# Other step numbers for weight sums, operand rows and output-weight conversions in the feed-forward part of a bucketed attention kernel

## The chip, the cores and the metric

The kernel runs on one core of one Trainium2 chip. The metric is the device time of one execution in microseconds; of the kernel before there are three timed runs and one profiled execution.

## What is computed

Four batches, eight heads, 768 positions of 64 dimensions go through an attention in which a query sees only the keys of its own hash bucket, and the 3072 resulting rows of 512 numbers go through two matrix products with a piecewise activation between them.

```python
q_bits = (np.einsum('bhsd,dk->bhsk', q, proj) > 0)           # 6 bits -> bucket, the same for k
scores = np.where(q_bucket[:, :, :, None] == k_bucket[:, :, None, :], scale * q @ k^T, -1e9)
attn   = softmax(scores);   x = (attn @ v), heads side by side       # 3072 x 512
h = x @ w_in                                                         # 512 -> 2048
g = np.where(h >= 1, h, np.where(h <= -1, 0.0, (h + 1) ** 2 / 4.0))
out = (g @ w_out).astype(np.float32)                                 # 2048 -> 512
```

The inputs and the result are fp32; w_in and w_out arrive as float64, seen as pairs of 32-bit words.

## The kernel before

TensorE takes the faster fp32r form, so each fp32 operand is split into a high part (a copy rounded to fp32r, made on ACT) and a low part (the rest, made on DVE), and each product is three matmuls: high by high, high by low, low by high.

The program is written out by hand: nothing is rescheduled, and each engine's instructions stand in the order in which the Python code makes them. The attention comes first and ends at about 474 us. The change is in the feed-forward part after it, in the lists `prep` and `post`: `prep[n]` holds the calls that are made ahead of step n's matmuls, `post[n]` those behind them. SP issues nearly all DMAs of this part, also in order, and a DMA that has to wait holds up every later one.

**Stage 1, steps n = 0 to 31** (`gemm1`, L799), on chunks 0 and 1 of 384 rows (batch 0). A step is 12 matmuls into one of two PSUM banks (`hb`, used in turn), then `act_in` (ACT, L633 and L634, two buffers for its first result `t`), `act_out` (DVE, L639 and L640), `g_hi` (ACT, L644) and `g_lo` (DVE, L648), and from step 3 on nine matmuls of the second product (L674, 128x512), which belong to the unit three steps earlier. Beside this stage run: the operand of chunk 1 (`xm.make`, L554, L557, L559 and L39, from rows `pcs` loaded from DRAM); the conversion of w_out blocks from float64 (`wo_steps`: load s0, DVE passes s1 to s4 on L70 to L82, ACT cast s5, DVE low part s6, block i's output weights needed at step `need`); the blocks 2 to 7 that the attention converted and parked in DRAM (`get`, L102); plain weight blocks put into the DRAM tiles `wc` (`w_plain`); the first weight sums (`w_plan`); and the operands of batch 1 (`x_plan(1, 0)` and `x_plan(1, 1)`).

**Stage 2, steps N1 + k with N1 = 32 and k = 0 to 167** (L891). Here two column chunks and two weight blocks are multiplied with seven block products instead of eight (a Strassen-type scheme). For each batch 1, 2, 3 there are eight groups i of seven products s = 0 to 6, so s = k mod 7. A product is six matmuls (L891) and then four to six of the second product's matmuls (L674). The seven results are combined thus: s0 is copied by ACT (L896), s1 (L898), s3 (L902), s4 (L904), s5 (L907) and s6 (L910) are added to or subtracted from earlier ones by DVE straight out of PSUM; s2, s4, s5 and s6 go through `act_in`, and the `act_out` of a product stands on DVE ahead of the next product's own L-line. PSUM has two banks for these products, so TensorE must wait until DVE has read an older product out of the bank: the bank for s6 is freed by L904, that for the next group's s0 by L907, and that for its s1 by L910.

Each product takes one block of weights from a ring of nine SBUF slots; `w_load` (L775) loads the block for product k + 8 at product k. Blocks 0 to 2 of a pair i are plain weights, blocks 3 to 6 are sums and differences, made once per pair by `w_plan(i, get, first, second, his, los, put)`: load the raw weights (`w_get`, L740 and L741), three DVE subtractions (`w_sum`, L39 on `sumw`; one of 512 columns at `first`, two of 256 at `second`), two ACT casts, two DVE low parts of 512 columns (at `los`), and two stores into `wc` (`w_put`, L756 and L757). In a group the order of blocks is 0, 5, 1, 4, 3, 6, 2.

The operands of batch b are made by `x_plan(b, cc, raw, er, norm, made)` in two halves cc: at `raw` the attention's rows are loaded (`x_raw`, L689 and L691), at `er[k]` two rows per head pair (a maximum's correction and a reciprocal sum) are loaded and spread over the partitions by a broadcasting DMA (`x_er`, L537, `t<-ed` or `wbig<-ed` in the profile), at `norm[k]` two DVE operations apply them (`x_norm`, L698 and L700), and at `made` follow sums (L709), ACT casts (L712) and, a step later, low parts (L39). `xm.sums_load`, `sums_add` and `sums_inv` make batch 3's reciprocal row sums.

Of the kernel before, what the change touches and what calls it, by code (L numbers as in the profile page):

```python
# [11 lines left out]
F32 = mybir.dt.float32  # L12
# [8 lines left out]
B, H, S, D = 4, 8, 768, 64  # L21
NB = 6
P = 128
# [4 lines left out]
DM = H * D  # L28
# [13 lines left out]
class WeightSplit:  # L42
# [10 lines left out]
    def steps(self, src, shape, hi, lo, cp, stage=None, low=None, keep=None):  # L53
        nc, n = self.nc, self.n
        st = {}

        def s0():
            st["raw"] = self.pool.tile([P, n, 2], I32, name="wraw")
            dst = st["raw"]
            if len(shape) == 4:  # L60
                dst = dst.rearrange("p (c f) t -> p c f t", c=shape[1])
            nc.sync.dma_start(out=dst, in_=src)

        def s1():
# [12 lines left out]
        def s3():  # L77
            nc.vector.scalar_tensor_tensor(out=st["a"], in0=st["raw"][:, :, 0], scalar=self.sc[:, 1:2],
                                           in1=st["a"], op0=ALU.logical_shift_right, op1=ALU.bitwise_or)

        def s4():
            nc.vector.scalar_tensor_tensor(out=st["sq"], in0=st["sq"], scalar=WMIN2,  # L82
                                           in1=st["a"].bitcast(F32), op0=ALU.is_ge, op1=ALU.mult)

        def s5():
            if cp is nc.scalar:
                cp.copy(out=hi, in_=st["sq"])
            else:
                cp.tensor_copy(out=hi, in_=st["sq"])

        def s6():
# [8 lines left out]
        def get():  # L100
            st["sq"] = self.pool.tile([P, n], F32, name="wsq")
# [470 lines left out]
    return steps  # L572


def ffn(ctx, tc, wpair, woh, wol, xm, xa, xb, areas, wst, wq, wc, out, prep, post):

# [46 lines left out]
    def at(n, fn, *a):  # L623
        prep[n].append((fn, a))
# [134 lines left out]
    def w_plan(i, get, first, second, his, los, put):  # L759
        at(get, w_get, i)  # L760
        at(first, w_sum, 0)
        at(second, w_sum, 1)
        at(second, w_sum, 2)
        for t in range(2):
            after(his[t], w_hi, t)
            at(los[t], w_lo, t)
        at(put, w_put, i)
# [16 lines left out]
            w_load(k)  # L784


    def load_x1(ct):
        if ct == 0:
            xm.load_sv(1, spc[0])
        xm.load_raw(1, ct, pc[ct])  # L790
# [14 lines left out]
        prep[0].insert(0, (load_x1, (ct,)))  # L805
    for ct in range(NCT):
        for part in range(4):
            n = (0, 2, 3, 5)[ct] + (0, 0, 0, 2)[part]
            (post if part == 2 else prep)[n].append((xm.make, (1, ct, part, *xs[1], [nc.vector] * 2)))
    for i in range(NFT // 2):  # L810
        at(8 + i, w_plain, i)
    for i in range(3):
        n = 17 + 4 * i
        w_plan(i, n, n + 2, n + 3, (n + 3, n + 3), (n + 4, n + 4), n + 5)
    w_plan(3, 29, 31, N1 + 1, (N1 + 1, N1 + 2), (N1 + 2, N1 + 3), N1 + 5)
    for i in range(4, NFT // 2):
        n = N1 + 8 * i - 28
        w_plan(i, n, n + 4, n + 5, (n + 5, n + 6), (n + 6, n + 7), n + 9)
    at(8, lambda: xm.sums_load(*(t[:, 0:NF] for t in pc[4:6]), B - 1))
    at(10, xm.sums_add)  # L820
    at(10, xm.sums_inv, B - 1)
    x_plan(1, 0, 11, (11, 12, 13, 14), (13, 14, 15, 16), (17, 17, 18, 18, 19, 19, 20))
    x_plan(1, 1, 22, (24, 24, 25, 25), (26, 26, 27, 27), (28, 28, 29, 29, 30, 30, 31))
    for b in (2, 3):
        for cc in range(2):
            t = N1 + 56 * (b - 2) + (7, 31)[cc]
            x_plan(b, cc, t, [t + k for k in range(4)], [t + 4 + k for k in range(4)],
                   [t + 9 + 2 * k for k in range(7)])

    at(27, ring_staged)  # L830
    for k in range(4, NRING):
        at(N1 + (k > 6), w_load, k)

# [102 lines left out]
def lsh_attn_ffn(ctx: ExitStack, tc: tile.TileContext, qk, v, pj, cv, w_in, w_out, out):  # L936
# [43 lines left out]
    def at(g, fn, *a):  # L980
        tasks[g].append((fn, a))
# [58 lines left out]
    attention(actx, tc, wst, T1, T2, qk, v, pj, cv, x_d, s_d, e_d, tasks, attn)  # L1040
    actx.close()

    wp2 = ctx.enter_context(tc.tile_pool(name="wp2", bufs=1, reuse_waits="tile"))
    for i in range(len(wo), NFT):
        woh.append(wp2.tile([P, DM], F32R, name=f"woh{i}"))
        wol.append(wp2.tile([P, DM], F32R, name=f"wol{i}"))
    for i in range(2, NFT):
        n = i + NFT - NW1
        need = i + GLAG if i < LEAD else 2 * i + GLAG + 1 - LEAD
        if n < NSTG:  # L1050
            get, cast, low = late[n]
            n_get, n_cast, n_low = i - (4 if i < 6 else 2), i - (2 if i < 6 else 1), i + (i > 5)
            if i < 4:
                prep[0] += [(cast, ()), (low, ())]
                continue
            prep[n_get].append((get, ()))
        else:
            need -= (i > 9) + (i > 11)
            *st, cast, low = wo_steps(i, nc.scalar, None, nc.vector)
            for fn, m in zip(st, (6, 4, 4, 3, 3)):  # L1060
                prep[need - m].append((fn, ()))
            n_cast, n_low = need - 3, need - 2
        post[n_cast].append((cast, ()))
        prep[n_low].append((low, ()))
    areas = [flat(t) for t in (T2[i0], T2[i1], T1[i0])], wbig.rearrange("p i t n -> p (i t n)")
    ffn(ctx, tc, wpair, woh, wol, xm, xa, xb, areas, wst, wq, wc, out, prep, post)


def _consts():
# [47 lines left out]
```

## Time and profile before

| What | us |
|---|---|
| median of 3 runs (1008.84 to 1012.06) | 1009.53 |
| the profiled execution's own time | 1011.32 |
| its span, first to last instruction | 1009.5 |
| TensorE busy in the span | 973.4 |
| DVE, ACT, POOL busy | 797.7, 680.9, 341.7 |

TensorE counts as busy for 96% of the span at a granted clock of full speed. How long a stretch without a stall takes is therefore read from the trace's rows by time, stretch by stretch: in stage 2 the same seven products come 24 times.

### The profile page before, as it was taken

What the parts mean: (1) busy time and instruction counts of PE and PEld (TensorE: products, weight loads), DVE (VectorE), ACT (ScalarE), POOL (GpSimd) and SP (SyncE); (2) the same over time, 40 slices, a digit from 0 to 9 for tenths busy, and PEclk for the clock granted to TensorE, in tenths of its full rate; (3) what the DMA queues carried; (4) which work ended last, traced back from release to release, by engine and by line L of the source; (5) the groups of instructions that cost most, each with busy time, mean ns of one, the idle gap of its engine ahead of it and who ended that gap; (6) DMA issues with size and microseconds to landing.
All of it is one profiled execution on the core that took longest, in us unless ns stands there. A gap on an engine that the chain in (4) does not pass through costs nothing.

```text
span 1009.5 us, 15524 instructions
## 1 busy us (share of the span) xinstructions
PE 973.4 (96%) x5036; PEld 889.6 (88%) x5036; DVE 797.7 (79%) x1356; ACT 680.9 (67%) x1489; POOL 341.7 (34%) x412
## 2 busy tenths in 40 slices
PE   5899999999999999999999999899999999999997
PEld 4789999999999999999899899678887888888886
DVE  7678999999999999885879986777766776655563
ACT  5778888998989988887655655454554545554443
POOL 6666777778877777666000000000000000000000
PEclk9999999999999999999999999999999999999999
DMA  2646677766666666635467577869458484454431
GB/s 90 166 110 155 168 189 189 190 173 173 173 156 167 173 176 176 155 111 146 131 206 254 159 227 236 243 218 252 115 146 231 118 214 116 126 169 122 116 84 62
DMA packets 94168, 166.18 MB, mean 165 GB/s; under 512 B 13832, under 2 KB 51336, under 8 KB 94088
## 3 DMA queue, kind: packets, MB, share of 16 engines
q1 hardware_dynamic: 93872, 165.19, 58.8%
q8 instruction: 40, 0.66, 0.3%
q14 instruction: 40, 0.33, 0.1%
q10 hardware_dynamic: 216, 0.00, 0.0%
HBM read 106.13 MB, written 33.87 MB: 139 GB/s over the span
## 4 chain that ended last, share of the span: by engine, by line
PE 76%; DVE 11%; ACT 5%; DMA 5%; issue 2%; SPq 1%; POOL 0%; ACTq 0%; DVEq 0%
PE y L674 18%; PE h L891 13%; PE smax L258 7%; PE o L332 6%; PE o L330 6%; PE s L298 6%; PE o L331 6%; PE s L297 6%; PE h L799 4%; DMA t<-ed 2%; PE o L178 2%; DVE nm L262 2%; DVE t L639 1%; ACT t L633 1%; ACT z L634 1%
## 5 line engine op out<-in xcount | busy, mean ns | idle before, releaser
L306 ACT ACTIVATE ph<-s 128x384 fp32r<-128x384 f32 x380 | 188.1, 495 | 47.1 <-PE s L298 40.2
L262 DVE TENSOR_REDUCE nm<-smax 128x1 f32<-128x768 f32 x186 | 176.2, 947 | 16.4 <-PE smax L258 14.7
L39 POOL TENSOR_TENSOR pl<-pf,ph 128x384 fp32r<-128x384 f32 x128 | 138.7, 1089 | 79.8 <-ACT pf L311 79.4
L639 DVE SCALAR_TENSOR_TENSOR t<-t 128x384 f32<-128x384 f32 x128 | 71.3, 557 | 109.6 <-ACT z L634 109.3
L39 DVE TENSOR_TENSOR pl<-s,ph 128x384 fp32r<-128x384 f32 x256 | 135.6, 545 | 14.5 <-ACT s L311 10.6
L297 PE MATMUL s<-t 128*128 128x384 f32 x384 | 132.1, 344 | 0.8 <-DVE t L212 0.8
L332 PE MATMUL o<-pl,va 128*128 128x386 f32 x384 | 130.3, 339 | 0.2 <-DVE pl L39 0.2
L330 PE MATMUL o<-ph,va 128*128 128x386 f32 x384 | 130.1, 339 | 0.0
L298 PE MATMUL s<-t 128*128 128x384 f32 x384 | 130.1, 339 | 0.0
L331 PE MATMUL o<-ph,vb 128*128 128x386 f32 x384 | 129.5, 337 | 0.0
L311 ACT ACTIVATE s<-s 128x384 f32<-128x384 f32 x252 | 125.3, 497 | 0.0
L674 PE MATMUL y<-t,ghi 128*128 128x512 f32 x384 | 124.7, 395 | 0.4 <-ACT ghi L644 0.4
L258 PE MATMUL smax<-t 128*128 128x384 f32 x372 | 102.1, 355 | 5.5 <-DVE nm L262 4.5
L644 ACT CAST ghi<-z 128x384 fp32r<-128x384 f32 x129 | 65.2, 505 | 36.8 <-DVE z L640 32.8
L891 PE MATMUL h<-wbig,t 128*128 128x384 f32 x399 | 82.2, 338 | 5.3 <-DVE wsq L910 2.4
L258 PEld LDWEIGHTS smax<-t 128*128 128x128 f32 x372 | 63.5, 188 | 23.8 <-DVE nm L262 22.6
L633 ACT ACTIVATE t<-wsq,mh 128x384 f32<-128x384 f32 x48 | 29.6, 617 | 79.9 <-DVE wsq L904 47.5
L891 PEld LDWEIGHTS h<-wbig,t 128*128 128x128 f32 x399 | 70.9, 188 | 12.9 <-DVE wsq L910 3.4
L634 ACT ACTIVATE z<-t,m 128x384 f32<-128x384 f32 x128 | 79.0, 617 | 4.2
L674 PEld LDWEIGHTS y<-t,ghi 128*128 128x128 f32 x384 | 71.3, 188 | 11.6 <-ACT ghi L644 0.9
L674 PE MATMUL y<-woh,glo 128*128 128x512 f32 x192 | 75.9, 395 | 1.1 <-DVE glo L648 1.0
L674 PE MATMUL y<-woh,ghi 128*128 128x512 f32 x192 | 75.6, 394 | 0.7 <-ACT ghi L644 0.7
(151 smaller groups left out, 2104.2 us busy)
## 6 DMA issues: line engine op xcount, KB each, us to landing
t<-wc SPq DMA_DIRECT2D x92, 256.0 KB
t<-t SPq DMA_DIRECT2D x60, 384.0 KB
wraw<-wc SPq DMA_DIRECT2D x76, 256.0 KB
raw<-in_qk_dram SPq DMA_DIRECT2D x15, 768.0 KB
wraw<-in_w_in_dram SPq DMA_DIRECT2D x16, 512.0 KB
wraw<-in_w_out_dram SPq DMA_DIRECT2D x16, 512.0 KB
xd<-xs SPq DMA_DIRECT2D x32, 192.5 KB
vraw<-in_v_dram SPq DMA_DIRECT2D x16, 384.0 KB
```

Of the source, the lines that this page charges most:

```text
L39: eng.tensor_tensor(out=out, in0=a, in1=b, op=ALU.subtract)
L258: nc.tensor.matmul(out=smax[hd][:, hf, 0:HS], lhsT=t2[:, 0, h, i * P:(i + 1) * P], rhs=t2[:, 1, h, hf * HS:(hf + 1) * HS], start=True, sto ...
L262: nc.vector.tensor_reduce(out=nmp(hd)[:, i:i + 1], in_=smax[hd][:, :, 0:HS], axis=AX.XY, op=ALU.max, negate=True)
L297: nc.tensor.matmul(out=ps[:, 0:HS], lhsT=t1[:, 1, h, ks], rhs=t1[:, 0, h, sl], start=True, stop=False)
L298: nc.tensor.matmul(out=ps[:, 0:HS], lhsT=t2[:, 1, h, ks], rhs=t2[:, 0, h, sl], start=False, stop=True)
L306: nc.scalar.activation(out=ph[:, 0:HS], in_=ps[:, 0:HS], func=AF.Exp, scale=SCALE)
L311: nc.scalar.activation(out=pf, in_=ps[:, 0:HS], func=AF.Exp, scale=SCALE)
L330: nc.tensor.matmul(out=o, lhsT=wa, rhs=ph, start=(jj == 0), stop=False)
L331: nc.tensor.matmul(out=o, lhsT=wb, rhs=ph, start=False, stop=False)
L332: nc.tensor.matmul(out=o, lhsT=wa, rhs=pl, start=False, stop=(jj == NJ - 1))
L674: nc.tensor.matmul(out=ys[c][m], lhsT=g_[:, m * P:(m + 1) * P], rhs=w, start=(first and k == 0), stop=(last and k == 2))
L891: nc.tensor.matmul(out=ps, lhsT=w[:, cs], rhs=x, start=(n == 0 and s not in (2, 3, 6)), stop=(n == 5), skip_group_check=True)
```

## The change

Only step numbers and one buffer change; the attention and all arithmetic stay.

- `w_plan`: pairs 0 and 1 are made in steps 21 to 31 instead of 17 to 26, pair 2 from step 30 to N1 + 5, and pairs 3 to 7 with a period of seven products instead of eight, so that each of its parts always falls on the same product of a group: load at s4, first subtraction at s1, second at s2, casts behind s2 and s3, low parts at s4, store at s5.
- `x_plan`: for batch 1 the first half starts three steps sooner; for batches 2 and 3 each call has its own lists. The spread rows are issued seven or more products ahead of their `norm`, which was four.
- Output weights not parked by the attention (blocks 8 to 15): `need` is two steps sooner for blocks 8 to 11 and one for 12 to 15, and every part of the conversion moves with it.
- Parked blocks 6 and 7 come back into halves of `sumw` (`sflat`) at steps 1 and 2, instead of into the pool `wsq` at 4 and 5.
- `xm.make` for the first column tile of chunk 1: the two DVE operations stand behind step 1's matmuls instead of ahead of step 0's, the rest a step later too.
- Batch 3's sums are loaded at N1 + 1 and inverted at N1 + 5 (were 8 and 10), the first four ring loads move from step 27 to 30.

```diff
-            n = (0, 2, 3, 5)[ct] + (0, 0, 0, 2)[part]
-            (post if part == 2 else prep)[n].append((xm.make, (1, ct, part, *xs[1], [nc.vector] * 2)))
+            n = (1, 2, 3, 5)[ct] + (0, 0, 0, 2)[part]
+            (post if part == 2 or ct == 0 and part < 2 else prep)[n].append(
+                (xm.make, (1, ct, part, *xs[1], [nc.vector] * 2)))
...
-    for i in range(3):
-        n = 17 + 4 * i
-        w_plan(i, n, n + 2, n + 3, (n + 3, n + 3), (n + 4, n + 4), n + 5)
-    w_plan(3, 29, 31, N1 + 1, (N1 + 1, N1 + 2), (N1 + 2, N1 + 3), N1 + 5)
-    for i in range(4, NFT // 2):
-        n = N1 + 8 * i - 28
-        w_plan(i, n, n + 4, n + 5, (n + 5, n + 6), (n + 6, n + 7), n + 9)
-    at(8, lambda: xm.sums_load(*(t[:, 0:NF] for t in pc[4:6]), B - 1))
-    at(10, xm.sums_add)
-    at(10, xm.sums_inv, B - 1)
-    x_plan(1, 0, 11, (11, 12, 13, 14), (13, 14, 15, 16), (17, 17, 18, 18, 19, 19, 20))
+    w_plan(0, 21, 24, 25, (25, 25), (26, 26), 27)
+    w_plan(1, 26, 28, 29, (29, 29), (30, 30), 31)
+    w_plan(2, 30, N1 + 1, N1 + 2, (N1 + 2, N1 + 3), (N1 + 4, N1 + 4), N1 + 5)
+    for i in range(3, NFT // 2):
+        n = N1 + NBLK * (i - 2)
+        w_plan(i, n - 3, n + 1, n + 2, (n + 2, n + 3), (n + 4, n + 4), n + 5)
+    x_plan(1, 0, 8, (8, 9, 10, 11), (11, 12, 13, 14), range(15, 22))
...
-    for b in (2, 3):
-        for cc in range(2):
-            t = N1 + 56 * (b - 2) + (7, 31)[cc]
-            x_plan(b, cc, t, [t + k for k in range(4)], [t + 4 + k for k in range(4)],
-                   [t + 9 + 2 * k for k in range(7)])
-
-    at(27, ring_staged)
+    x_plan(2, 0, N1 + 6, range(N1 + 6, N1 + 10), [N1 + n for n in (13, 14, 17, 20)],
+           [N1 + n for n in (21, 24, 27, 28, 31, 34, 35)])
+    x_plan(2, 1, N1 + 37, [N1 + n for n in (28, 30, 32, 34)], [N1 + n for n in (41, 42, 44, 46)],
+           range(N1 + 47, N1 + 54))
+    N3 = N1 + 56
+    x_plan(3, 0, N3 + 8, range(N3 + 8, N3 + 12), [N3 + n for n in (15, 16, 18, 22)],
+           [N3 + n for n in (23, 25, 26, 28, 30, 31, 32)])
+    x_plan(3, 1, N3 + 34, [N3 + n for n in (26, 28, 30, 32)], [N3 + n for n in (37, 39, 43, 44)],
+           [N3 + n for n in (46, 47, 48, 50, 51, 53, 54)])
+    at(N1 + 1, lambda: xm.sums_load(*(t[:, 0:NF] for t in pc[4:6]), B - 1))
+    at(N1 + 5, xm.sums_add)
+    at(N1 + 5, xm.sums_inv, B - 1)
+
+    at(30, ring_staged)
...
-            n_get, n_cast, n_low = i - (4 if i < 6 else 2), i - (2 if i < 6 else 1), i + (i > 5)
+            n_cast, n_low = i - (2 if i < 6 else 1), i + (i > 5)
...
-            prep[n_get].append((get, ()))
+            if i < 6:
+                prep[i - 4].append((get, ()))
+            else:
+                staged.append(lambda t, get=get, i=i: prep[i - 5].append((get, (t[:, (i - 6) * DM:(i - 5) * DM],))))
         else:
-            need -= (i > 9) + (i > 11)
+            need -= 2 + (i > 9)
```

How this moves instructions is shown at three places. The first is DVE from its first instruction of stage 1: L554 and L557 are `xm.make`, L639 and L640 `act_out`, L648 `g_lo`. Before:

```order
L554 SCALAR_TENSOR_TENSOR pcs<-t_2_79,xsva,pcs 128x384
L557 TENSOR_TENSOR pcs<-pcs,t_2_79 128x384
L639 SCALAR_TENSOR_TENSOR t<-t 128x384
L640 TENSOR_TENSOR z<-t,z 128x384
L639 SCALAR_TENSOR_TENSOR t<-t 128x384
L640 TENSOR_TENSOR z<-t,z 128x384
L648 TENSOR_TENSOR glo<-z,ghi 128x384
```

and now:

```order
L639 SCALAR_TENSOR_TENSOR t<-t 128x384
L640 TENSOR_TENSOR z<-t,z 128x384
L639 SCALAR_TENSOR_TENSOR t<-t 128x384
L640 TENSOR_TENSOR z<-t,z 128x384
L554 SCALAR_TENSOR_TENSOR pcs<-t_2_79,xsva,pcs 128x384
L557 TENSOR_TENSOR pcs<-pcs,t_2_79 128x384
L648 TENSOR_TENSOR glo<-z,ghi 128x384
```

The first two activations stand ahead of the two operations on loaded rows; ACT's cast L559, which reads their result, stands behind step 1's `act_in` instead of step 0's.

The second is DVE in stage 2 where batch 2's first `x_norm` operations stand (L698 and L700, with `xsva`), from the s3 of a group (L902, now L909) to its s6 (L910, now L917). Before, in the group k = 7 to 13:

```order
L39 TENSOR_TENSOR sumw<-sumw,tmp 128x512
L902 TENSOR_TENSOR wa<-h_6045,wsq 128x384
L39 TENSOR_TENSOR sumw<-sumw,tmp 128x512
L698 SCALAR_TENSOR_TENSOR pcs<-t_2_79,xsva,pcs 128x384
L700 TENSOR_TENSOR pcs<-pcs,t_2_79 128x384
L904 TENSOR_TENSOR wsq<-h_6046,wa 128x384
L648 TENSOR_TENSOR glo<-z,ghi 128x384
L639 SCALAR_TENSOR_TENSOR t<-t 128x384
L640 TENSOR_TENSOR z<-t,z 128x384
L698 SCALAR_TENSOR_TENSOR pcs<-wbig,xsva,pcs 128x384
L700 TENSOR_TENSOR pcs<-pcs,wbig 128x384
L907 TENSOR_TENSOR wa<-wa,h_6045 128x384
```

and in the same group now:

```order
L909 TENSOR_TENSOR wa<-h_6045,wsq 128x384
L39 TENSOR_TENSOR sumw<-sumw,tmp 128x512 x2
L911 TENSOR_TENSOR wsq<-h_6046,wa 128x384
L648 TENSOR_TENSOR glo<-z,ghi 128x384
L639 SCALAR_TENSOR_TENSOR t<-t 128x384
L640 TENSOR_TENSOR z<-t,z 128x384
L914 TENSOR_TENSOR wa<-wa,h_6045 128x384
L639 SCALAR_TENSOR_TENSOR t<-t 128x384
L640 TENSOR_TENSOR z<-t,z 128x384
L698 SCALAR_TENSOR_TENSOR pcs<-t_2_79,xsva,pcs 128x384
L700 TENSOR_TENSOR pcs<-pcs,t_2_79 128x384
L917 TENSOR_TENSOR wsq<-h_6046,wsq 128x384
```

The `x_norm` pairs that stood ahead of s4, s5 and s6 in one group are now ahead of s6 (k = 13), s0 (14), s3 (17) and s6 (20); both low parts of the weight sums stand together ahead of s4.

The third is SP in the last part of the weight sums, pair 6 (`wc_103`), with batch 2's second half of spread rows (`ed_69`) and row loads (`xd_61`). Before:

```order
L756 DMA wc_103<-tmp 128x4x256
L757 DMA wc_103<-sumw 128x4x256
L775 DMA wraw<-wc_102 128x512 x2
L691 DMA pcs<-xd_61 128x2x384 x2
L537 DMA t_2_79<-ed_69 64x2x384 x2
L775 DMA t_1_75<-wc_102 128x512
L537 DMA wbig<-ed_69 64x2x384 x2
L775 DMA t_1_75<-wc_102 128x512
L537 DMA wbig<-ed_69 64x2x384 x2
L775 DMA t_1_75<-wc_103 128x512
```

and now:

```order
L537 DMA wbig<-ed_69 64x2x384 x2
L775 DMA t_1_75<-wc_102 128x512
L756 DMA wc_103<-tmp 128x4x256
L757 DMA wc_103<-sumw 128x4x256
L775 DMA t_1_75<-wc_103 128x512
L537 DMA t_1_75<-ed_69 64x2x384 x2
L775 DMA t_2_76<-wc_103 128x512 x2
L775 DMA wraw<-wc_103 128x512
L691 DMA pcs<-xd_61 128x2x384 x2
```

Between the store of pair 6 and the first ring load of that pair stood four other ring loads, and now none; the first of the two loads of `t_2_76` now is the first that reads a stored sum. The spread rows now stand ahead of the row load.

More of the change, by code (lines that the diff above doesn't have):

```diff
@@ L98, in steps, with get @@
             return [s0, s1, s2, s3, s4, s5, s6] + ([put] if keep is not None else [])
-        def get():
-            st["sq"] = self.pool.tile([P, n], F32, name="wsq")
+        def get(sq=None):
+            st["sq"] = self.pool.tile([P, n], F32, name="wsq") if sq is None else sq
             nc.sync.dma_start(out=st["sq"], in_=stage)
@@ L572, in ffn_order, with ffn @@
     return steps
-def ffn(ctx, tc, wpair, woh, wol, xm, xa, xb, areas, wst, wq, wc, out, prep, post):
+def ffn(ctx, tc, wpair, woh, wol, xm, xa, xb, areas, wst, wq, wc, out, prep, post, staged):
     nc = tc.nc
@@ L784, in ring_staged @@
             w_load(k)
+    for get in staged:
+        get(sflat)
     def load_x1(ct):
@@ L1041, in lsh_attn_ffn @@
     actx.close()
+    staged = []
     wp2 = ctx.enter_context(tc.tile_pool(name="wp2", bufs=1, reuse_waits="tile"))
@@ L1065, in lsh_attn_ffn @@
     areas = [flat(t) for t in (T2[i0], T2[i1], T1[i0])], wbig.rearrange("p i t n -> p (i t n)")
-    ffn(ctx, tc, wpair, woh, wol, xm, xa, xb, areas, wst, wq, wc, out, prep, post)
+    ffn(ctx, tc, wpair, woh, wol, xm, xa, xb, areas, wst, wq, wc, out, prep, post, staged)
 def _consts():
```

## Prediction

> **What bounds the kernel now.** I read the page first, then windows cut where stalls begin and end, then the waits of TensorE and DVE after the attention.
>
> ```profile
> span 1009.5 us, 15524 instructions
> PE 973.4 (96%) x5036; PEld 889.6 (88%) x5036; DVE 797.7 (79%) x1356; ACT 680.9 (67%) x1489; POOL 341.7 (34%) x412
> ```
>
> TensorE is the bound, and its matmuls are not touched. A change of order can only win back time in which it stands idle, so I look for that from 474 us on.
>
> ```profile
> 474.22:605.50 131.28, 128.89 (x646) 115.92 (x646) 108.67 (x206) 75.53 (x145) 2.55 (x2) 1.00 0.63 193
> 605.50:709.85 104.35, 96.77 (x467) 83.20 (x465) 76.35 (x150) 50.73 (x97) 0.00 (x0) 1.00 0.80 233
> 756.93:791.40 34.47, 32.07 (x157) 27.91 (x156) 22.31 (x44) 15.55 (x30) 0.00 (x0) 1.00 0.76 201
> 791.40:980.00 188.60, 188.60 (x937) 169.06 (x936) 119.35 (x234) 93.32 (x175) 0.00 (x0) 1.00 0.49 137
> ...
> 620.59:657.59 37.00, 32.49 (x157) 27.92 (x156) 27.41 (x54) 16.86 (x33) 0.00 (x0) 1.00 0.93 265
> ```
>
> The columns are length, then busy time (and count) of PE, weight loads, DVE, ACT, POOL, then granted clock, DMA share and GB/s. The row from 791.40 is 84 products without a stall: 188.60 / 84 = 2.245 us each, 15.72 us a group of seven. The row from 605.50 is 42 products, at that pace 94.3 us, less 0.7 because products 3 to 5 carry four second-stage matmuls instead of five: 93.6. It took 104.35: **10.75 us lost**, of which the two groups from 620.59 (k = 7 to 20) lose 37.00 - 31.43 = 5.6. The row from 756.93 is 14 products, 31.43 us, and took 34.47: **3.04 lost**. What was waited for:
>
> ```profile
> PE h L891 <- DVE wsq L910: 4.6, 4, 1.6
> PE h L891 <- DVE wa L907: 2.2, 2, 1.4
> PE h L799 <- ACT t L633: 1.3, 1, 1.3
> ...
> DVE pcs L698 <- DMA t<-ed: 3.5, 1, 3.5
> ...
> DVE pcs L698 <- DMA wbig<-ed: 2.3, 1, 2.3
> ```
>
> (total us, times, longest). TensorE's rows name DVE or ACT, late in emptying a PSUM bank, and none names a ring slot's load; DVE in turn stood for spread rows. In stage 1 the pace without a stall is that of the second and third row here (the first is used further down):
>
> ```profile
> 476.66 2.87 DMA pcs<-xd
> 490.60 2.11 PE h L799 x12
> 492.71 2.10 PE y L674 x9
> ```
>
> 32 first products and 29 second ones of 2.10 us are 128.1 us against 131.28: **3.2 lost**. All in all 17.0 us are to be had, and no more.
>
> **Why DVE is late.** An undisturbed group in the chain of waits:
>
> ```profile
> 740.01 1.38 PE y L674 x6
> 744.66 1.16 PE y L674 x5
> 750.24 1.06 PE h L891 x6
> 751.33 0.57 DVE wsq L904
> 751.92 0.63 ACT t L633
> 754.37 0.48 DVE wa L907
> 757.32 0.48 DVE wsq L910
> ```
>
> Product s4 ends on TensorE at 751.30, and DVE's reading of s6 at 757.80, 6.50 us later, because L904, L907 and L910 are tied through two ACT passes and an `act_out` each. TensorE wants the bank that L910 frees after 1.16 + (1.06 + 1.16) + (1.06 + 1.38) + (1.06 + 1.16) = 8.04 us. **The cover is 1.55 us**, and whatever else stands on DVE ahead of L907 or L910 is paid from it. Ahead of L904 there is room of its own: the `act_out` of s2 ends 2.45 us (751.92 to 754.37, the same steps) after s2 does, which is 4.44 - 2.45 = 2.0 before s4 ends; L902 takes 0.47, so 1.5 us are free.
>
> The stalled group, from the same view and, in the last two rows, DVE's timeline:
>
> ```profile
> 626.35 7.44 DMA t<-ed
> 641.53 4.64 DMA wc<-sumw
> 660.73 1.31 PE h L891 x6
> ...
> 633.93 0.62 DVE L698 SCALAR_TENSOR_TENSOR pcs<-t,xsva,pcs 128x384 f32<-128x384 f32 x1 [3.55 <-DMA t<-ed]
> 635.06 0.55 DVE L904 TENSOR_TENSOR wsq<-h,wa 128x384 f32<-128x384 f32 x1
> ```
>
> The spread rows landed 7.44 us after their issue, DVE stood at L698, and L904 came behind it. Two more `x_norm` pairs (1.13 us each, as from 633.93 to 635.06) stood ahead of L907 and L910. Batch 3 repeats it at 761. Behind a stall the first six matmuls take 1.31 instead of 1.06: a refill costs 0.25.
>
> **The change part by part.**
>
> *Spread rows seven products ahead, `x_norm` moved.* SP's own rows:
>
> ```profile
> 622.39 1.36 SPq L775 DMA_DIRECT2D t<-wc  x2
> ...
> 639.47 0.32 SPq L775 DMA_DIRECT2D wraw<-wc  x1
> ```
>
> From the ring loads at 622.39 to the spread rows at 626.35 SP needed 4.0 us; with 7.44 that is 11.4 of the 15.7 us that seven products last, and no other `er` list of batches 2 and 3 is nearer. So the wait at L698 goes. The pairs now stand at s6, s0, s3, s6 (batch 2) and s1, s2, s4, s1 (batch 3): 1.13 at s6 is under the cover of 1.55, at s4 under the 1.5, and at s0 to s2 nothing that TensorE soon waits for is behind it. This takes the 3.04 and the 5.6.
>
> A page of the Trainium skill speaks against this part. "DMA: Bandwidth & Descriptors", section "Anatomy of one DMA", gives a fixed 2.0 us plus bytes over 436 GB/s (fitted on another issue path); for 192 KB that is an estimated 2.45 us, four products of lead would have been plenty, and without the 5.8 us of waits at L698 to win the sum would be about -10. The 7.44 above, behind row loads in the same queue, disagrees.
>
> *Weight sums in step with the groups.* Durations from DVE's timeline, start to start:
>
> ```profile
> 553.19 0.55 DVE L639 SCALAR_TENSOR_TENSOR t<-t 128x384 f32<-128x384 f32 x1
> 553.78 0.56 DVE L640 TENSOR_TENSOR z<-t,z 128x384 f32<-128x384 f32 x1
> 554.25 0.55 DVE L648 TENSOR_TENSOR glo<-z,ghi 128x384 fp32r<-128x384 f32 x1
> 554.72 0.75 DVE L78 SCALAR_TENSOR_TENSOR wa<-wraw,wsc,wa 128x512 int32<-128x512 int32 x1
> ...
> 556.11 0.69 DVE L39 TENSOR_TENSOR sumw<-tmp 128x512 f32<-128x512 f32 x1
> 556.71 1.02 DVE L39 TENSOR_TENSOR wbig<-pcs,wbig 128x384 fp32r<-128x384 f32 x2
> ```
>
> A 512-column subtraction is 0.60 us, a 384-column one 0.47. With a period of eight products the parts wandered over the group and met L907 and L910 too; now the two low parts (1.20) are always ahead of L904 (1.5 free), the subtractions at s1 and s2. That takes the other 5.1 of the 10.75. Where work meets: at k = 17 a pair puts L902 off by 1.13, so the low parts at 18 end 2.0 - 1.13 - 0.47 - 1.20 = 0.8 too late, and the pair at k = 20 adds 1.13: 1.9 against 1.55. **One stall of 0.4 is left at k = 22, 0.7 with its refill.** The operands' own sums and low parts (0.47 each) put at most 1.4 into one group's s4 to s6, under the cover.
>
> *Stores close ahead of their loads.* A pair's store at s5 is now two products, 4.65 us, ahead of the first load that reads it. SP took 2.1 us from a ring load (639.47) to the second store (641.53), and that landed after 4.64: SP will stand some 2.1 us per group. The load has eight products, 17.7 us, until its use. Cost taken: 0; bounds 0 and, at a landing of 16 us, 3.2 us in each of six groups (rivals).
>
> *Row loads.* For batch 3's second half the row load is three products (6.9 us) ahead. Its landing has no row; between 2.87 us (476.66, half the size) and 7.44, with 1.2 us of issue, DVE waits 0 to 1.8 us, at an s2, in front of the 2.0 us. I take 0 and keep 2 for the range.
>
> *Stage 1.*
>
> ```profile
> 480.90 0.51 ACT L559 CAST t<-pcs 128x384 fp32r<-128x384 f32 x1 [3.00 <-DVE pcs L557]
> 530.15 0.62 DVE L698 SCALAR_TENSOR_TENSOR pcs<-tmp,xsvb,pcs 128x384 f32<-128x384 f32 x1 [3.35 <-DMA tmp<-ed]
> 565.72 0.50 PE L674 MATMUL y<-woh,glo 128*128 128x512 f32 x1 [0.99 <-DVE glo L648]
> ```
>
> ACT stood 3.00 us at L559 for DVE, which stood for the row load, and TensorE's fourth step paid 1.3 plus some refill. Now both activations come first: 1.4 gone. Later DVE lost 3.35 us to spread rows two steps ahead, and stayed behind until `g_lo` was late at 565.72 and around it: 1.8. Now they are three steps ahead. The sooner conversions make steps 11 to 14 the fullest: 1.53 of base (0.59 + 0.47 + 0.47), a pair of 1.13, and by turns 1.39 (554.72 to 556.11) or about 1.7 (three passes) of conversion, 4.05 and 4.4 against 4.20 a step. That fills DVE and does not pile up; from step 15 on it is lighter, since the weight sums went from 19 to 24. Step 26 holds 1.53 + 1.20 + 2.26 = 5.0 and step 25 only 2.3, and TensorE needs `g_lo` a step later. The 3.2 come back; if the lead of three steps failed too, 1.8 of it would not. I keep 0.3 for refills.
>
> **Sum.** -10.75 - 3.04 - 3.2 + 0.7 + 0.3 = -16.0. The profiled execution took 1011.32 us (its span and 1.8 around it), so 995.3; it lies 1.79 above the median 1009.53, which gives **993.5 us**, 1.6% faster.
>
> **Rivals.** *Only the DMA waits go.* DVE's work is as much as before, 73% of the window from 605.50. If low parts still meet L907 and L910 (ACT's casts behind s2 and s3 could hold them up), the 5.1 and the 1.8 stay lost: 993.5 + 6.9 = 1000.4. Against: in the new order nothing but batch 3's sums (under 0.9 us, once) stands at s5 up to k = 53.
>
> *Waits move.* DMA is busiest (0.93 in the row from 620.59) just where the new leads begin; if rows issued sooner land as much later, the waits come back in other products and only stage 1's 3.2 are won: 1006.3. Against: each landing in the rows is under half of the new lead.
>
> *Slower.* The stores. If a stored pair lands so late that the load behind it, and every later SP issue with it, overruns the ring, TensorE waits in each of the groups 2 to 7. From a load landing like the slowest row, 7.44, this decides from a store's landing of about 4.65 - 2.1 + 17.7 - 7.44 = 12.8 us; at 16 us it is 3.2 us in six groups, 19.2, and the time 1009.53 - 16.0 + 19.2 = 1012.7. The one landing seen, 4.64, is far below. The same DMA page says that a completion can take surprisingly long when the target is HBM, and these stores go there.
>
> **Chances.** Forecast 0.74, only DMA waits 0.16, moved waits 0.06, slower 0.04. Changes under 0.3% (3 us) could not be told from none. Faster by more are the first two and part of the third, less a little for what I overlook: 0.88; same 0.07; slower 0.05. The range reaches from 990.5 (all 17.0 won, and a us or two between runs) to 1001.5, past the first rival.
>
> **What would show it.** Right: groups of 15.7 us from k = 7 on, no wait of DVE for spread rows, no 1.3 us at TensorE's fourth step, one short wait near k = 22, ring loads on SP 2 us behind stores. Wrong: TensorE waiting for a ring slot's load, DVE waiting for `pcs<-xd`, or stalls that stay in the groups up to k = 41.

## The result and the profile after

The changed kernel takes 1005.19 us (median of 6 runs, 1004.07 to 1005.65); the kernel before took 1010.27 beside it (6 runs). The ratio is 0.9943, with a 95% interval of 0.9925 to 0.9961: 0.6% faster, a good third of the 1.6% that were forecast. The profiled execution took 1005.65 us.

From the page of the profile after:

```profile
span 1003.9 us, 15529 instructions
PE 972.9 (97%) x5036; PEld 891.9 (89%) x5036; DVE 794.0 (79%) x1356; ACT 680.7 (68%) x1489; POOL 344.3 (34%) x412
```

TensorE's busy time is what it was, as it must be. The stretches that answer to those of the prediction, cut again at the first matmuls of a group (length, PE, weight loads, DVE, ACT, POOL, granted clock, DMA share, GB/s):

```profile
472.96:600.87 127.91, 127.91 (x646) 116.15 (x646) 104.89 (x197) 74.14 (x143) 2.55 (x2) 1.00 0.56 178
600.87:704.74 103.87, 97.82 (x466) 85.67 (x465) 75.97 (x151) 52.44 (x99) 0.00 (x0) 0.97 0.85 255
631.89:655.66 23.77, 18.40 (x79) 16.16 (x78) 14.59 (x29) 8.35 (x15) 0.00 (x0) 0.86 0.88 272
704.74:753.17 48.43, 48.04 (x235) 41.92 (x234) 35.88 (x72) 26.55 (x51) 0.00 (x0) 1.00 0.47 137
753.17:784.64 31.47, 31.47 (x157) 28.20 (x156) 20.81 (x41) 14.79 (x28) 0.00 (x0) 1.00 0.80 220
```

Stage 1 (first row) no longer stalls: 127.91 against 131.28. Neither does the first half of batch 3 (last row): 31.47 against 34.47. But k = 0 to 41 (second row) takes 103.87 against 104.35, nearly as before, and one group in it, k = 14 to 20 (third row), takes 23.8 where an undisturbed one takes 15.7. Group by group, from the start of a group's first matmul to the next group's (k = 42 to 62 are groups 6 to 8, the fourth row):

```
group      k      before  after
1         7-13     19.14  15.96
2        14-20     17.86  23.78
3        21-27     17.05  15.75
4        28-34     17.48  16.18
5        35-41     17.73  17.15
6 to 8   42-62     47.08  48.43
9, 10    63-76     34.49  31.47
12,15,16           47.08  48.01
```

What TensorE waited for from 470 us on, and behind it the one DMA wait of DVE's between 600 and 660 us (total us, times, longest):

```profile
PE h L898 <- DVE wsq L905: 5.8, 2, 5.4
PE y L674 <- ACT ghi L644: 0.7, 1, 0.7
PE h L898 <- DVE wsq L917: 0.6, 2, 0.3
```

```profile
DVE sumw L39 <- DMA wc<-sumw: 5.0, 1, 5.0
```

DVE's waits for spread rows (3.5 and 2.3 us before) are gone, and a new one has come: the first weight subtraction of pair 4 (k = 15) waits until the store of pair 3 (k = 12) has left `sumw`, the buffer that it overwrites. The chain of waits (its longer pieces) shows how that store came to be late, and the timeline of SP's queue what stood ahead of it:

```profile
621.34 6.65 DMA t<-ed
628.01 8.32 DMA t<-ed
636.39 6.45 DMA wc<-sumw
643.48 0.56 DVE wsq L905
644.08 2.29 PE h L898 x6
```

```profile
616.83 1.13 SPq L664 DMA_DIRECT2D out_dram<-ot  x2
...
620.69 1.26 SPq L537 DMA_DIRECT2D t<-ed  x2
...
632.76 0.55 SPq L740 DMA_DIRECT2D tmp<-wq  x1
...
636.39 0.37 SPq L757 DMA_DIRECT2D wc<-sumw  x1
```

Product 12 began at 627.2. Its store went out at 636.39, because SP's issue of one spread row followed the landing of an earlier one and the store followed that of the next. It landed 6.45 us later. The spread rows of batch 2 (`t<-ed`, `wbig<-ed`) had been issued early and were in time; the store behind them paid. SP was behind even ahead of them: product 6 began at 613.47, its spread rows went out at 620.69, after output stores (L664) which had waited 3.8 us in all for ACT's copies. The DMA engines were full:

```profile
629.00:633.00 4.00, 4.00 (x22) 3.64 (x21) 2.60 (x6) 1.64 (x3) 0.00 (x0) 1.00 1.09 228
...
637.00:641.00 4.00, 1.72 (x9) 1.14 (x7) 0.92 (x2) 1.20 (x2) 0.00 (x0) 1.00 1.08 385
...
644.00:648.00 4.00, 3.92 (x11) 3.53 (x12) 3.90 (x10) 1.35 (x3) 0.00 (x0) 0.50 0.84 271
```

The last row shows a second loss: after the idle time the granted clock was 0.50, and the six matmuls of product 17 took 2.29 us, against 1.31 after the stalls of before. Products 16, 17 and 18 took 7.75, 4.22 and 2.68 us, 8.0 more than three undisturbed ones; 5.37 of it was idle time, **the rest, 2.6 us, is slow clock and refill**.

### The profile page after: what moved, and what is told of

The parts are those of the page before. It is cut to its first block, busy times and chain, and to the rows that moved or that the text cites. A ratio compares the mean times of both kernels' runs of the same rounds, so it can differ in the third digit from the quotient of the medians.

```text
span 1003.9 us, 15529 instructions
## 1 busy us (share of the span) xinstructions
PE 972.9 (97%) x5036; PEld 891.9 (89%) x5036; DVE 794.0 (79%) x1356; ACT 680.7 (68%) x1489; POOL 344.3 (34%) x412
## 4 chain that ended last, share of the span: by engine, by line
PE 84%; DVE 6%; ACT 4%; DMA 3%; issue 1%; SPq 0%; POOL 0%; ACTq 0%; DVEq 0%
PE y L674 23%; PE h L898 15%; PE smax L258 7%; PE h L802 7%; PE o L332 6%; PE s L298 6%; PE o L330 6%; PE o L331 6%; PE s L297 6%; DMA t<-ed 2%; PE o L178 2%; DVE nm L262 2%; DMA wc<-sumw 1%; ACT t L633 1%; DVE nm L359 1%
## 5 line engine op out<-in xcount | busy, mean ns | idle before, releaser
L39 POOL TENSOR_TENSOR pl<-pf,ph 128x384 fp32r<-128x384 f32 x128 | 141.7, 1112 | 79.1 <-ACT pf L311 78.6
L639 DVE SCALAR_TENSOR_TENSOR t<-t 128x384 f32<-128x384 f32 x128 | 71.3, 557 | 115.4 <-ACT z L634 115.2
L633 ACT ACTIVATE t<-h,mh 128x384 f32<-128x384 f32 x56 | 32.5, 581 | 77.1 <-PE h L802 48.3
```

The source lines that it names most:

```text
L39: eng.tensor_tensor(out=out, in0=a, in1=b, op=ALU.subtract)
```

## The experiments

The theory: the rows' traffic makes the store late; what is forecast of DVE is right as far as it goes. The rivals: three products are too short for the store whatever the traffic; the weight sums' new places are to blame; the small new losses (groups 4 to 8, 12, 15, 16) have a cause outside DVE. All ratios are against the kernel before (1010.4 to 1011.6 beside them).

### Rows with an eighth of the columns

```diff
 def x_er(b, cc, k):
+    # for (2, 0): columns 0:48 of 384 of each spread row, same number of DMAs
```

> The changed kernel, but of batch 2's first half each spread row is loaded over 48 columns instead of 384 (an eighth of the bytes; the rest of the row is left as it was, so that half's operands are not the reference's). Same number of DMAs, same DVE work. Theory 'full queue': the rows issued at k = 6 to 9 fill the DMA engines, SP is held up, pair 3's store is issued 9 us late and lands 6.45 us after that, and the next pair's first subtraction waits 4.95 us for it; with an eighth of the bytes the wait and the stall at k = 17 (7.75 and 4.22 us instead of 2.21) go, about -8, near 997 us. Rival 'distance': three products between a pair's store and the next pair's overwriting of the same buffer are too few by themselves; the wait stays within 1 or 2 us of 4.95, time 1003 to 1005.

Measured: 1001.79 us (one run). TensorE's wait at k = 16 fell from 5.37 to 1.91 us and group 2 to 17.97. So the rows' bytes make most of the lateness. That something is left speaks for neither side, since everything else that SP issues in that stretch was unchanged: the store still went out 4.7 us after product 12 began (632.48 and 627.8), where it was 9.2 in the changed kernel.

### Another buffer for the store

```diff
-        o = sum_w[...]                      # all pairs
+        o = two idle output tiles           # pair 3 only
```

> The changed kernel, but pair 3's sums are made in two buffers of their own (two output tiles that are idle then), so the next pair's first subtraction has nothing to wait for; DMA traffic is the same, one store more. Both 'full queue' and 'distance': the 4.95 us wait at k = 15 goes, TensorE's stall at k = 17 with it, near 997 us, with the store landing as late as now (6 us or more after an issue at 636). Rival 'DVE pile': the two operand pairs at k = 13 and 14 and the subtractions behind them are late by themselves; then a stall of 2 us or more stays at k = 15 to 17, time 1002 or more.

Measured: 1001.84 us (4 runs), ratio 0.9917 (0.9902 to 0.9932). 3.4 us won over the changed kernel, but the place did not become clean. The waits from 600 to 660 us:

```profile
PE h L911 <- DVE wsq L918: 2.5, 1, 2.5
DVE sumw L39 <- DMA tmp<-wq: 2.1, 1, 2.1
DVE sumw L39 <- DMA wc<-sumw: 0.5, 1, 0.5
```

(L918 here is L905.) With the buffer free, the same subtraction waited for the next thing in the full queue: pair 4's raw weights. The time and the stall of 2.5 us are nearly those that the rival "DVE pile" named, but DVE stood idle for a transfer there and was not behind with work.

### Sums of before with rows of after, and the reverse

```diff
-    w_plan(0, 21, ...) ... period 7        # first run: the lists of before, period 8
-    x_plan(2, 0, N1 + 6, ...) ...          # second run: batches 2 and 3 as before
```

> The changed kernel with the weight sums at the step numbers of the kernel before (period of eight products), all else as changed. 'Full queue': a store (pair 4, at k = 13) still falls behind the same rows and the next sum is again three products later, so a wait of some us on the store stays at about k = 16, and the parts that meet L907 and L910 come back: 1006 to 1009. Rival 'the new places of the sums made the stall': it goes, 999 to 1002.

> The changed kernel with batch 2's and 3's operand lists of the kernel before (spread rows four products ahead of their use), weight sums as changed. If the places of the sums bring the 5.1 us that I forecast for them and stage 1 its 3.4: 1010.3 - 8.5 = 1001.8, with the waits of DVE for spread rows back (3.5 and 2.3 us). If the places of the sums bring nothing: 1007. If the stores wait here too, as 'distance' has it: 1007 to 1010.

Measured: with the old sums 1005.86 us (4 runs), ratio 0.9957 (0.9942 to 0.9972), so the new places of the sums are worth some 0.7 us; the stall is there too, on a later store, which was issued with the old plan at k = 13:

```profile
648.41 2.29 PE L899 MATMUL h<-wbig,wraw 128*128 128x384 f32 x6 [4.33 <-DVE wa L910]
```

With the old rows 1009.91 us (10 runs), ratio 0.9992 (0.9982 to 1.0002): nothing is won at all. DVE waits for spread rows as before, and groups 1 to 5 take 91.7 us against 89.3. It waits for a store too, as the last of the three outcomes had it: in group 5 (19.44 us, 17.73 before) the store of pair 6 (k = 33) went out behind the old rows of batch 2's second half. DVE stood 1.2 us for it and TensorE 1.96, with slow matmuls behind:

```profile
681.08 6.64 DMA t<-ed
687.78 7.47 DMA wc<-sumw
...
697.60 2.24 PE h L894 x6
```

Pair 3's store was 9.0 us behind its product here as well (636.95 and 627.9), but by then the group was late for want of rows, and DVE did not wait for that store. Stage 1's gain is in this run too (product 0 at 601.56 instead of 605.53), and most of it is given back in groups 1 to 5. **Old sums or old rows alone do not cure it: in all three kernels a store falls behind spread rows in the queue.** What the rows' lead and the sums' places are worth once no store is late, the split rows below tell.

### Rows spread out in time

```diff
-    x_plan(2, 0, N1 + 6, range(N1 + 6, N1 + 10), ...)
+    x_plan(2, 0, N1 + 1, [N1 + n for n in (1, 3, 6, 8)], ...)
```

> The changed kernel with the spread rows of batch 2's first half issued at products k=1, 3, 6 and 8 instead of 6 to 9, and the raw rows at k=1 instead of 6. Same transfers, same bytes, only nothing of them stands ahead of the store of k=12 any more. Theory (the store is late because the DMA engines are full from 616 to 640 us): the store of k=12 is issued within 2 us of its product and lands in about 5, the wait at k=16 falls from 5.4 us to under 1, the granted clock stays at 1.00, group 2 takes 16 to 17 us instead of 23.8, and the time comes to 997 to 999. Rival (three products are too short for that store whatever the traffic, since 2.4 us were left when the rows carried an eighth of their bytes): 2 to 2.5 us of wait stay at k=16, group 2 takes 18 to 20, 1000.5 to 1002. Second rival (the rows now collide with the loads at the start of stage 2 and wait there): group 0 or 1 grows by over 1 us.

> The rows of the run before (k=1, 3, 6, 8), and the sums of pair 3 in two tiles of their own, so that nothing has to wait for that store. Theory (full engines make every transfer late, the store and the raw weights of the next pair alike): no wait over 0.5 us is left in group 2, which takes 16 us, and the time comes to 996.5 to 998.5; if the rows alone have cured it, within 1 us of the run before. Rival (the distance of three products is what binds): this run wins 2 us or more over the run before.

Measured: 1002.04 us (4 runs), ratio 0.9908 (0.9893 to 0.9923). The wait at the store is gone (group 2: 16.37), its buffer unchanged: three products are enough. But something else was late, earlier, as the second rival had it. TensorE's and ACT's timelines:

```profile
619.79 0.73 PE L674 MATMUL y<-t,ghi 128*128 128x512 f32 x2 [1.72 <-ACT ghi L644]
...
653.68 1.31 PE L898 MATMUL h<-wbig,t 128*128 128x384 f32 x6 [0.99 <-DVE wsq L917]
```

```profile
618.74 0.58 ACT L663 COPY ot<-y 128x512 f32<-128x512 f32 x1 [1.73 <-DMA out_dram<-ot]
```

An output tile had not yet been written out when ACT needed it. With own tiles for pair 3 on top of it: 1001.83 us (4 runs), ratio 0.9903 (0.9886 to 0.9919), no difference. The tiles were taken from just those that the output needs, so the first of these waits grew to 2.28 us; the run says nothing more of the distance. The second wait is the stall at k = 22 that the prediction foresaw: 0.99 us of idle time, and product 21 takes 1.16 us more than an undisturbed one. In the changed kernel it does not show, probably because DVE and ACT caught up during the stall at k = 16.

### Rows on both sides of the store

```diff
-    x_plan(2, 0, N1 + 6, range(N1 + 6, N1 + 10), [N1 + n for n in (13, 14, 17, 20)], ...)
+    x_plan(2, 0, N1 + 1, [N1 + n for n in (1, 8, 13, 14)], [N1 + n for n in (13, 14, 17, 19)], ...)
```

> The changed kernel with the spread rows of batch 2's first half issued two ahead of the crowded stretch (k=1 and 8) and two behind the store of k=12 (k=13 and 14), and the last norm at k=19 instead of 20. Theory (the DMA engines are asked for more than they move between 612 and 636 us, and whatever is issued last then is late: the store in the changed kernel, the output flush when the rows came at k=1, 3, 6, 8): with half of the rows' bytes on either side neither is late; group 1 takes 16.0, group 2 16.0 to 16.5 and group 3 16 (the norm no longer stands ahead of the last read of its group), the clock stays at 1.00, 996 to 998.5. Rival (the rows of k=13 and 14, only four and five products ahead, now come late themselves): waits of the norm for its rows at k=17 or 19, 1 to 4 us in group 2, 998.5 to 1002.

Measured: 1000.50 us (4 runs), ratio 0.9901 (0.9885 to 0.9918), the best but for the next one, its equal. No wait of TensorE's over 0.5 us is left from 600 to 700 us, group 1 takes 15.96, groups 2 and 3 16.79 and 16.69, and the clock stays at 1.00. Four and five products of lead were enough: DVE waits for no spread row, the sign that the rival named. The expected 996 to 998.5 was still missed; groups 2 and 3 keep a loss of about 1 us each. **The stall was the crowd in the queue.**

### The same, with the old weight sums

```diff
     x_plan(2, 0, N1 + 1, [N1 + n for n in (1, 8, 13, 14)], ...)
-    w_plan(0, 21, ...) ... period 7
+    w_plan as before, period 8
```

> The run with the rows split (k=1, 8, 13, 14), and the weight blocks made at the places of the kernel before: with no store in TensorE's way this tells what the new places of the weight sums are worth by themselves. The prediction put 5.1 us on them: then groups 1 to 5 take 5 us more than in the run with the rows split and the time is 1005 to 1006. Rival (the sums only stand in other products, and VectorE's work around them is the same): groups 1 to 5 take 0.5 to 1.5 us more, as groups 4 and 5 did in the changed kernel with the old sums (16.7 and 17.6 against 16.2 and 17.2), 1000.5 to 1002. Second rival: the store of k=13, whose buffer is overwritten at k=16, is late again with the rows issued right beside it, a wait of 2 to 5 us at k=16 to 18.

Measured: 1000.49 us (4 runs), ratio 0.9898 (0.9879 to 0.9917), the same time. Groups 1 to 5 and then 6 to 8, of the run with the new sums and of this one, and groups 1 to 5 of the kernel before:

```profile
615.61:698.42 82.81, 81.07 (x391) 69.82 (x390) 65.77 (x130) 45.57 (x86) 0.00 (x0) 1.00 0.82 262
...
698.42:746.78 48.36, 48.00 (x235) 41.93 (x234) 35.83 (x72) 26.57 (x51) 0.00 (x0) 1.00 0.48 137
```

```profile
616.70:700.39 83.69, 80.93 (x391) 69.86 (x390) 63.97 (x126) 44.35 (x84) 0.00 (x0) 1.00 0.86 247
...
700.39:748.51 48.12, 47.75 (x236) 42.02 (x235) 35.62 (x71) 26.57 (x51) 0.00 (x0) 1.00 0.46 130
```

```profile
620.59:709.85 89.26, 81.68 (x392) 69.60 (x390) 67.33 (x133) 43.18 (x83) 0.00 (x0) 1.00 0.84 242
```

With everything but the new weight sums, the split rows above all, 89.26 - 83.69 = 5.57 us are won (4.15 of it in groups 1 and 2, 37.00 against 16.07 + 16.78). The weight sums in step bring 0.88 in groups 1 to 5 and lose 0.24 behind them: **0.6 us, where 5.1 were forecast**, and by the medians nothing.

### Is it DVE that costs the rest?

```diff
 def x_lo(b, cc, o):
+    # small low parts: for batches 2 and 3 columns 0:48 of 384 only
+    # on GpSimd (on top of the split rows): the whole of them there
 x_plan(2, ...)
+    # other products (on top of the run with own tiles): the lists of `made`
```

> The changed kernel, with the low parts of batch 2's operands made for 48 of 384 columns only (the rest of these low parts holds old values, so the products of batch 2 are not the reference's): 14 VectorE subtractions of about 0.5 us become about 0.1 us each, nothing else changes. Theory (small losses come from VectorE's queue ahead of its reads): groups 4 to 8, 81.8 us together against 78.5 without loss, come to 79 to 80, the time 1002.5 to 1003.5; the wait of k=16 stays as it is. Rival (they don't come from VectorE): groups 4 to 8 stay at 81.5 to 82.

The kernel did this to batch 3 too, 28 low parts in all, which the text above does not say. For the next one the run before is that with own tiles for pair 3, for the one behind it that with the split rows.

> The run before, and the operands of batch 2 made at products 20, 21, 24, 27, 28, 31, 33 (instead of 21, 24, 27, 28, 31, 34, 35) and 45, 46, 48, 49, 50, 52, 53 (instead of 47 to 53), so that VectorE has one operand less to make in products 34 to 36 where the output weights' sums also fall. Theory (the small losses of 0.3 to 1.5 us in groups 4 to 8 are VectorE falling behind ahead of its reads): group 5 falls from 17.2 us to 16.2 or less, 0.7 to 1.5 us are won over the run before: 995.5 to 997.5. Rival (they are TensorE's or the DMA's own): groups 4 to 8 keep their times, no difference.

> The run before, and the low parts of the operands of batches 2 and 3 made on GpSimd, which does nothing else in stage 2, instead of VectorE (28 subtractions of about 0.5 us less on VectorE). Theory (the small losses of groups 4 to 8, 12, 15 and 16, some 4 us together, are VectorE falling behind ahead of its reads, as the run with small low parts showed): these groups come to 15.7 to 15.8, 3 to 4 us are won over the run before. Rival (GpSimd is slow, and the sums made in place have to wait for it, or its accesses slow VectorE's): VectorE's instructions beside it take longer or wait for GpSimd, and less than 1.5 us is won, or some is lost.

Measured with the small low parts: 999.82 us (one run). Groups 4 to 8 of the changed kernel, and of this one:

```profile
671.42:753.17 81.75, 80.67 (x391) 69.71 (x390) 62.73 (x125) 45.17 (x87) 0.00 (x0) 1.00 0.64 187
```

```profile
669.72:748.25 78.53, 78.53 (x391) 70.39 (x390) 58.06 (x124) 44.81 (x86) 0.00 (x0) 1.00 0.64 194
```

Not one stall is left there (78.5 is five times 15.7). The time is better than forecast, because the stall at k = 16 did not stay as it was: 3.74 us of idle time, group 2 at 21.35. So the small losses are DVE's, though in that window it is busy for only 77% of the time (62.73 of 81.75). Where they arise, in DVE's timeline of the changed kernel at k = 36:

```profile
692.52 0.55 DVE L39 TENSOR_TENSOR t<-pcs,t 128x384 fp32r<-128x384 f32 x1
692.99 0.55 DVE L709 TENSOR_TENSOR pcs<-pcs 128x384 f32<-128x384 f32 x1
693.46 0.55 DVE L648 TENSOR_TENSOR glo<-z,ghi 128x384 fp32r<-128x384 f32 x1
693.93 0.68 DVE L39 TENSOR_TENSOR sumw<-tmp 128x512 f32<-128x512 f32 x1
694.53 0.55 DVE L39 TENSOR_TENSOR t<-pcs,t 128x384 fp32r<-128x384 f32 x1
695.00 0.55 DVE L905 TENSOR_TENSOR wsq<-h,wsq 128x384 f32<-128x384 f32 x1
```

Ahead of s1's read (L905) stand, without a gap, two low parts, an operand's sum, a `g_lo` and a weight subtraction, and TensorE's s3 waits 0.46 us for that read.

Operands at other products: 1003.04 us (4 runs), ratio 0.9918 (0.9901 to 0.9934), not better than the 1001.83 it started from. Group 5 did fall, from 17.17 to 16.61 us, but groups 3, 4 and 7 rose, and groups 3 to 8 together went from 98.95 to 99.22: the loss moved. The expected gain was missed.

On GpSimd: 1003.75 us (4 runs), ratio 0.9930 (0.9916 to 0.9945), 3.3 us slower than the run it started from; the rival holds. DVE's groups from 680 to 740 us without and with GpSimd beside it (busy, mean ns):

```profile
L640 DVE TENSOR_TENSOR z<-t,z 128x384 f32<-128x384 f32 x15 | 8.4, 558 | 0.5
...
L709 DVE TENSOR_TENSOR pcs<-pcs 128x384 f32<-128x384 f32 x6 | 3.3, 549 | 0.0
...
L917 DVE TENSOR_TENSOR wsq<-h,wsq 128x384 f32<-128x384 f32 x4 | 2.2, 548 | 0.0
```

```profile
L640 DVE TENSOR_TENSOR z<-t,z 128x384 f32<-128x384 f32 x15 | 11.3, 750 | 0.5
...
L709 DVE TENSOR_TENSOR pcs<-pcs 128x384 f32<-128x384 f32 x6 | 4.9, 822 | 0.0
L917 DVE TENSOR_TENSOR wsq<-h,wsq 128x384 f32<-128x384 f32 x4 | 2.2, 549 | 0.0
```

### What idle time does to the clock

```diff
+    # in front of s1's read in groups 18 to 22:
+    # 6, 8, 10, 12 and 16 subtractions on a tile that is no longer used
```

> The changed kernel with idle VectorE work put ahead of one of its reads in groups 18 to 22, which had no stall: 6, 8, 10, 12 and 16 subtractions of about 0.65 us on a tile that nothing reads any more. About 2 us of each is hidden, so TensorE should stand idle for about 2, 3, 4.5, 6 and 8 us. Theory (the clock falls after a long enough idle stretch, since 1.6 us left it at 1.00 in the kernel before and 5.4 us took it to 0.50 in the changed one): up to some length between 2 and 5 us a stall costs its own length and no more, and from there on 2 to 3 us more, whatever its length. Rival (the clock falls with anything that happens to TensorE's load over a longer time, or it fell for another reason): all five cost their own length, or the extra grows with the idle time.

Measured: 1038.01 us (one run). TensorE's timeline (in brackets the idle time before):

```profile
903.70 1.31 PE L904 MATMUL h<-wbig,wraw 128*128 128x384 f32 x6 [1.71 <-DVE wsq L911]
922.89 1.33 PE L904 MATMUL h<-wbig,wraw 128*128 128x384 f32 x6 [3.16 <-DVE wsq L911]
943.55 2.29 PE L904 MATMUL h<-wbig,t 128*128 128x384 f32 x6 [4.60 <-DVE wsq L911]
968.01 2.29 PE L904 MATMUL h<-wbig,t 128*128 128x384 f32 x6 [6.14 <-DVE wsq L911]
995.13 2.29 PE L904 MATMUL h<-wbig,t 128*128 128x384 f32 x6 [9.07 <-DVE wsq L911]
```

After 1.71 and 3.16 us six matmuls take 1.3 us, after 4.60 and more 2.29. Against the same groups of the changed kernel these five grew by 2.0, 3.4, 7.2, 8.5 and 11.6 us, that is by the idle time and 0.3, 0.3, 2.6, 2.4 and 2.5. The theory holds in this ladder; other runs narrow it (below).

## Why the prediction was wrong

**Right.** Stage 1: 3.2 forecast, 3.4 won; no part of it was tested alone, but it takes 127.9 us with the old weight sums too, so these have no share in it. Batch 3's first half: 3.04 forecast, 3.02 won. The spread rows: no wait of DVE for them is left, and once nothing else is in the way 5.57 us are won in groups 1 to 5 without the new sums; the forecast of 5.6 was for groups 1 and 2, where it is 4.15. The stall near k = 22 exists in the run with rows spread out (1.16 against 0.7).

**First failed step: "Stores close ahead of their loads", with "Cost taken: 0".** It counted only who reads what the store writes. That part came out nearly right: SP stood 16.7 us in five waits behind the stores from 600 to 720 us, 3.3 each against 2.1, and TensorE never waited for a ring load. The buffer that the store reads is overwritten too, three products behind (k = 12 to 15), and that term was missing. The old sums left the same three products; what changed is what stands ahead of it in SP's queue. The prediction quoted the DMA share of 0.93 there, and set the landings against the rows' own new lead, as if only they had a due time. It cost 8.0 us in the profiled execution: 5.4 of idle time, and 2.6 of slow clock and refill, where the sum knew only a refill of 0.25. The rival "waits move" (1006.3) comes nearest in time and kind, but the waits did not come back at the rows; they fell on the next transfer with a due time: a store, or raw weights when the store had another buffer, or an output tile when the rows were issued sooner. That its number is so near is partly luck: batch 3's 3.0 us, which it counts as lost, were won, and slow clock and small losses took their place.

**Second failed step: "Weight sums in step", 5.1 us.** They won about 0.6, and nothing by the medians. The 5.1 was got by subtraction: whatever of the 10.75 was not the rows' was put down to the sums. The run with small low parts shows that it is DVE's whole work between reads: groups 4 and 5 lose nothing there (31.39 us, twice 15.7, against 35.21 before). The prediction's cover looked at the reads of s4, s5 and s6 and said that at s0 to s2 "nothing that TensorE soon waits for is behind it"; the read of s1 is, as the rows of k = 36 show. With DVE that full, moving an operation moved the stall. This is the reason of the rival "only the DMA waits go" (DVE's work is as much as before): once no store is late, the time is 1000.5, where it has 1000.4, though partly by luck, since stage 1's 1.8, which it counts as lost, were won.

**A term left out.** Groups 6 to 8, 12, 15 and 16 had no stall before, and lose 1.35 and 0.93 us after. The new lists of the operands make it: with the old ones, in the run with old rows, these groups take 47.34 and 47.16 us, and with small low parts 47.14 and 47.08. Which of the new places does it was not tested; those at other products, spaced out, still lost 1.27 in groups 6 to 8.

**The balance** of the two profiled spans: -3.4 (stage 1), -3.0 (groups 9 and 10), -0.4 (groups 1 to 5), +2.3 (the groups just named) make -4.6 before rounding; the attention, whose code is the same, ended 1.26 us sooner, and some 0.2 were lost in the rest: 5.7 in all, 1009.53 to 1003.87.

Not settled: how long the stall at the store is from run to run. The same stretch took 21.35 to 23.78 us in the profiled executions that left it in place, and the split rows win 6.8 us by the spans, but 4.7 by the medians.

## What to carry to other kernels

A transfer that is issued sooner takes its place in a queue away from others: list every transfer of the stretch with its due time, and count as a due time also the moment at which the buffer that a store reads is overwritten. Where the DMA engines were already full, it helped to put bytes on both sides of the crowd rather than all of them ahead. And a gain got as a remainder (all losses less the ones explained) is no estimate of what the next edit wins; where DVE was full between its reads, moving work moved the stall, and only less work removed it.

## What the runs showed of the hardware

*The clock.* In stage 2 of all runs together idle stretches of up to 1.92 us were never followed by slow matmuls, those from 3.74 us on always. Between them it went both ways: 3.16 us left the clock at 1.00 in the ladder, while slow matmuls followed 1.96 and 2.18 us in the run with old rows, 2.28 in that with rows spread out and own tiles, and 2.46 in that with another buffer. Two of them:

```profile
632.48 2.00 PE L894 MATMUL h<-wbig,t 128*128 128x384 f32 x6 [2.18 <-DVE wsq L907]
```

```profile
641.72 2.29 PE L911 MATMUL h<-wbig,t 128*128 128x384 f32 x6 [2.46 <-DVE wsq L918]
```

So length alone does not decide. The Trainium skill, "TensorE: Matmul & The Clock Gate", section "Part 1: The HAM clock gate (the "warmup" mystery)", tells of an activity window of some 3.4 us that runs freely, and of half speed after an idle one. Half speed agrees with the 0.50 in the rows, and a window that runs freely would explain why both happen; but 1.96 to 2.46 us are shorter than the window, so it cannot have to be idle throughout. This was not tested by itself.

*GpSimd beside VectorE.* In the rows above VectorE's operations with two operands in SBUF took 750 and 822 ns on average instead of 558 and 549, the read of PSUM (L917) 549 and 548. The Trainium skill, page "SBUF — State Buffer", section "SBUF: two separate sides", says that these two engines share one pair of ports under a lock, which binds VectorE where it has two SBUF inputs. The rows agree.

*Full DMA engines at little throughput.* In the changed kernel the engines were equally full at 228 GB/s (629 to 633 us, where spread rows were under way) and at 385 (637 to 641): a stretch of this kernel must be judged by its DMA share, not by its bytes. What makes the difference is open: in the run with split rows the engines moved 372 GB/s (628 to 632, share 1.06) with spread rows under way too.
